# Attention backward, dV and dK: 32-row by 64-column matmul tiles and output tiles of one head per partition

## The chip, the core and the metric

The kernel runs on one core of one Trainium2 chip. The time is the device time of one execution in microseconds. Before the change it is 706.23 us, the median of three runs (704.14 to 710.16).

The core has a matrix engine (PE; its weight loads are listed apart as PEld), three engines for elementwise work (DVE, ACT, and POOL, which is GpSimd), a queue that only issues transfers here (SP), and 16 DMA engines that move data between HBM and the on-chip memory SBUF. Matmuls write PSUM, 8 banks of 512 fp32 values per partition, and ACT or DVE copy from there to SBUF.

## The reference

It is grouped-query attention with its gradients: 32 batches, 32 query heads with 4 queries each, 4 key/value heads, 2,048 keys, head size 128, all in bf16. Per batch and key/value head there are 8 x 4 = 32 query rows, so the four heads together fill 128 partitions.

```python
def _fwd_reference(q, k, v):
    ...
    scores = jnp.einsum("bhqd,bhkd->bhqk", q, k) * scale
    p = _softmax(scores, axis=-1)
    return jnp.einsum("bhqk,bhkd->bhqd", p, v)
...
def reference(q, k, v, grad_out):
    ...
    _out, _vjp = jax.vjp(_f, q, k, v)
    _grads = _vjp(grad_out)
    _out0 = jnp.asarray(_out)
    return (_out0, *[jnp.asarray(_g) for _g in _grads])
```

Written out per head, with e the exponentials and l their row sums: O = (e / l) V, dV = (e / l)^T dO, dS = e (dO V^T - delta) with delta the row sum of O dO, dQ = dS K scale / l, and dK = dS^T Q scale / l.

## The kernel before

One batch is some 60 steps, and the steps of several batches are interleaved in an order written out by hand: `STEADY` lists one round, where a suffix (`+`, `-`) says that a step belongs to a later or an earlier batch, and `TAIL` lists the last rounds. The engines carry out their instructions in the order in which these steps issue them; semaphores hold back an instruction whose input or buffer is not ready.

The steps of one batch:

- `LOAD` (L112): SP issues q, dO, four k and four v transfers of 512 KB. Key p x 16 + c lies in partition p, slot c, so a row of a transfer is 16 keys of one head, 4 KB. k has three buffers, v two; a load waits until PE is done with the old contents.
- `KT0..7`, `VT0..7` (L141 to L153): eight PE transposes each and a DVE copy. `QDT` does the same for q and dO.
- `Sa`, `Sb` (L155, L169): the scores; `EXa`, `EXb`: the exponentials on ACT; `NRM` (L197): 1/l on DVE, then on POOL dO / l (`dop`) and q scale / l (`qp`).
- `ETa/b`, `dSTa/b` (L208): transposes of e and dS; `O`, `dQ` (L222 to L253): gathers of 64 matmuls with 32 columns each, four column tiles at a time, and a small store on POOL's queue.
- `dPa`, `dPb` (L297): dO V^T on PE and dS on DVE.
- `dV0..7`, `dK0..7` (`outer`, L255): the pieces that the change is about. A piece covers two of the 16 key slots for all four heads. The array is used as two halves of 64 rows, and each half holds two heads. So that a half gives both heads side by side, `paired` (L190) lays `dop` and `qp` out as 256 columns, zero where the other head of the pair stands: four POOL operations of 32 partitions for each. A piece is four matmuls of 64 rows, 128 columns and 256 moving columns (L266); the two halves write one PSUM bank each. Then one copy of 128x1024 from PSUM to the output tile (L270), by ACT except where `TAIL` marks a step with `d`, for DVE.

The output tile of dV or dK has 128 partitions, 4 heads, 16 slots, 128 values: 32 KB per partition, three buffers for both. When its eight pieces are copied, POOL issues two stores of 1 MB, two heads each, in rows of 4 KB (L289). In the last batch half a tile leaves at a time, in one store each (L282). POOL's queue therefore holds, per batch, the `dop` and `qp` operations, the stores of O and dQ, and four large stores.

Of the kernel before, what the change touches and what calls it, by code (L numbers as in the profile page):

```python
# [9 lines left out]
BF16 = mybir.dt.bfloat16  # L10
ACT = mybir.ActivationFunctionType
ALU = mybir.AluOpType
# [49 lines left out]
def kernel(ctx: ExitStack, tc: tile.TileContext, q, k, v, grad_out, out_0, out_1, out_2, out_3):  # L62
    nc = tc.nc
    B, Hq, Sq, D = q.shape
    NH, Sk = k.shape[1], k.shape[2]
    P = 128
    G = Hq * Sq // NH
    C = Sk // P
    assert D == P and Hq * Sq == P and NH == 4 and G == 32 and C == 16
    scale = float(D) ** -0.5  # L70
    NZ = 3

    const = ctx.enter_context(tc.tile_pool(name="const", bufs=1))
    k_pool = ctx.enter_context(tc.tile_pool(name="kp", bufs=3))
# [7 lines left out]
    out_pool = ctx.enter_context(tc.tile_pool(name="outp", bufs=3))  # L82
    io_pool = ctx.enter_context(tc.tile_pool(name="iop", bufs=4))
    sm_pool = ctx.enter_context(tc.tile_pool(name="smp", bufs=3))
    ps_pool = ctx.enter_context(tc.tile_pool(name="ps", bufs=1, space=bass.MemoryType.PSUM))

    banks = Banks(ps_pool.tile([P, 8, 512], FP32, name="banks"))
# [3 lines left out]

    pairs = {}
    for x in ("dop", "qp"):
        for z in range(NZ):
            pairs[x, z] = const.tile([P, 2, D], BF16, name=f"{x}{z}")
            nc.gpsimd.memset(pairs[x, z][:], 0.0)

    q_f = q.rearrange("b h s d -> b (h s) d")  # L100
    go_f = grad_out.rearrange("b h s d -> b (h s) d")
    o_f = out_0.rearrange("b h s d -> b (h s) d")
    dq_f = out_1.rearrange("b h s d -> b (h s) d")
    k_v = k.rearrange("b h (p c) d -> b h p (c d)", c=C)
    v_v = v.rearrange("b h (p c) d -> b h p (c d)", c=C)
    dk_v = out_2.rearrange("b h (p c) d -> b p h (c d)", c=C)
    dv_v = out_3.rearrange("b h (p c) d -> b p h (c d)", c=C)

    store = nc.gpsimd
    st = {}  # L110
# [76 lines left out]
        )  # L187
        banks.give(t)

    def paired(S, name, src, by, b):  # L190
        t = pairs[name, b % NZ]
        for h in range(NH):
            r = slice(G * h, G * h + G)
            nc.gpsimd.tensor_scalar(out=t[r, h % 2, :], in0=src[r, :], scalar1=by[r, :], scalar2=None, op0=ALU.mult)  # L194
        S[name] = t

    def NRM(b):  # L197
        S = st[b]
        ls = sm_pool.tile([P, 1], FP32, name="ls")
        nc.vector.tensor_tensor(out=ls[:], in0=S["l"][:, 0:1], in1=S["l"][:, 1:2], op=ALU.add)  # L200
        S["rinv"] = sm_pool.tile([P, 1], FP32, name="rinv")
        nc.vector.reciprocal(out=S["rinv"][:], in_=ls[:])
        paired(S, "dop", S["do"], S["rinv"], b)
        S["srinv"] = sm_pool.tile([P, 1], FP32, name="srinv")
        nc.gpsimd.tensor_scalar_mul(out=S["srinv"][:], in0=S["rinv"][:], scalar1=scale)
        paired(S, "qp", S["q"], S["srinv"], b)

    def turned_rows(S, src, pool, name, i):  # L208
        t, ps = bank16()
# [44 lines left out]

    def outer(S, x, y, dst, name, i, b, copy):  # L255

        if name not in S:
            S[name + "left"] = 8
            S[name] = out_pool.tile([P, NH, C, D], BF16, name=name, tag="outp")
        t = banks.take(2)  # L260
        ps = banks.ap(t).rearrange("p a (j c d) -> p a j c d", j=2, c=2)
        for c in range(2):
            u = P * ((2 * i + c) % 8)
            for a in range(2):
                r = slice(2 * G * a, 2 * G * a + 2 * G)
                nc.tensor.matmul(  # L266
                    ps[:, a, :, c, :], lhsT=S[f"{x}{i // 4}"][r, u:u + P], rhs=S[y][r, :, :],
                    start=True, stop=True, tile_position=(2 * G * a, 0),
                )
        copy(  # L270
            out=S[name][:, :, 2 * i:2 * i + 2, :].rearrange("p h c d -> p h (c d)"),
            in_=banks.ap(t).rearrange("p a (j w) -> p (a j) w", j=2),
        )
        banks.give(t)
        S[name + "left"] -= 1
        if b == B - 1:

            half = f"{name}half{i // 4}"
            S[half] = S.get(half, 4) - 1
            if S[half] == 0:  # L280
                c = slice(8 * (i // 4), 8 * (i // 4) + 8)
                store.dma_start(  # L282
                    out=dst[b].rearrange("p h (c d) -> p h c d", d=D)[:, :, c, :].rearrange("p h c d -> p h (c d)"),
                    in_=S[name][:, :, c, :].rearrange("p h c d -> p h (c d)"),
                )
        elif S[name + "left"] == 0:
            o = S.pop(name)
            for a in range(2):
                store.dma_start(out=dst[b][:, 2 * a:2 * a + 2, :], in_=o[:, 2 * a:2 * a + 2].rearrange("p h c d -> p h (c d)"))  # L289

    def dV(b, i, copy=nc.scalar.copy):
        outer(st[b], "e", "dop", dv_v, "dv", i, b, copy)

    def dK(b, i, copy=nc.scalar.copy):
        outer(st[b], "ds", "qp", dk_v, "dk", i, b, copy)
# [21 lines left out]
    for w in STEADY.split():  # L317
        ahead = 0
        for mark, n in (("+3", 3), ("+2", 2), ("+", 1), ("-", -1)):
            if w.endswith(mark):  # L320
                w, ahead = w[:-len(mark)], n
# [3 lines left out]
    with tc.manual_schedule():  # L325
# [5 lines left out]
        for w in TAIL.split():  # L331
            w, b = w.split("@")
# [31 lines left out]
```

## Time and profile before

The page describes one profiled execution. Its span, first to last instruction, is 705.0 us, 1.2 us under the median of the three runs.

| | |
|---|---|
| median of three runs | 706.23 us |
| profiled execution, span | 705.0 us |
| chain that ended last | DMA 63%, PE 28%, DVE 3%, ACT 2% |
| L266 matmuls for dV, mean of one | 1,024, 274 ns |
| L266 matmuls for dK, mean of one | 1,024, 278 ns |
| L266 weight loads, mean of one | 94 to 95 ns |
| L270 copies on ACT, mean of one | 503, 1,021 to 1,026 ns |
| L194 `dop` and `qp` on POOL, mean of one | 256, 600 and 608 ns |
| L289 stores on POOL, mean of one issue | 124, 706 to 715 ns |
| k loads, v loads, issue to landing (median) | 13.9 us, 17.2 us |
| dV stores, dK stores, issue to landing (median) | 14.5 us, 11.1 us |

How to read it: a matmul's duration includes the time in which it passes through the array, so several are under way at once and the mean of one is not what it adds to the time; the distance between starts is. Busy shares are means over the whole span. DMA rates are given by slices of a fortieth of the span, 17.6 us each. A row of a timeline or of a chain gives start, length, engine, line, operation, output and input, and how many instructions were merged; in brackets stands the engine's idle time before it and what ended it.

### The profile page before, as it was taken

The page shows a single profiled execution, that of the slowest core. Times are in us where ns is not written, and L with a number is a line of the kernel's source. Part 1 is how long each engine was busy: PE and PEld are TensorE (multiplying, and loading weights), DVE is VectorE, ACT ScalarE, POOL GpSimd, SP SyncE. Part 2 cuts the span into 40 slices and gives each one's busy share as a digit, 9 for nine tenths or more (in the row PEclk, how much of TensorE's full clock was granted, in tenths as well). Part 3 has the DMA queues.
Part 4 walks back from the last instruction along what each step waited for, and adds up shares of the span by engine and source line. Part 5 has one row for each costly group of instructions (what it writes and reads, how often), then busy time and mean ns, then how long its engine had stood idle before and what let it go on. Part 6 is the DMA issues. An engine that isn't in the chain of part 4 may idle for free.

```text
span 705.0 us, 28195 instructions
## 1 busy us (share of the span) xinstructions
PE 634.6 (90%) x12352; PEld 458.4 (65%) x12352; DVE 596.3 (85%) x1001; ACT 560.6 (80%) x664; POOL 291.7 (41%) x492
## 2 busy tenths in 40 slices
PE   5899999799989799997999998979999989999893
PEld 4677777477767477764677766667666667666562
DVE  5999999789979869987788988859898879999983
ACT  0698898689879678886888897958988869887882
POOL 1445443344523444433444334533345443345451
PEclk9999999999999989999999999989999999999997
DMA  8999999999999999999999999999999999999867
GB/s 329 401 327 413 415 413 414 416 381 409 414 415 388 412 353 412 413 412 401 331 413 414 415 412 412 397 358 386 413 416 413 402 383 368 414 412 399 350 262 264
DMA packets 83067, 274.46 MB, mean 389 GB/s; under 512 B 16384, under 2 KB 16384, under 8 KB 82944
## 3 DMA queue, kind: packets, MB, share of 16 engines
q1 hardware_dynamic: 46080, 136.34, 50.0%
q0 software_dynamic: 36864, 136.33, 48.2%
q8 instruction: 96, 1.57, 0.8%
q14 instruction: 27, 0.22, 0.1%
HBM read 136.31 MB, written 136.31 MB: 387 GB/s over the span
## 4 chain that ended last, share of the span: by engine, by line
DMA 63%; PE 28%; DVE 3%; ACT 2%; issue 2%; POOL 1%; SPq 1%; POOLq 0%; ACTq 0%; DVEq 0%
DMA k_sb<-in_k_dram 27%; DMA v_sb<-in_v_dram 24%; PE banks L144 12%; DMA do_sb<-in_grad_out_dram 7%; PE banks L266 7%; PE banks L227 4%; PE banks L211 3%; PE banks L161 2%; DMA out_dram<-dk 2%; DMA out_dram<-dv 2%; ACT dv L270 1%; DVE ds L301 1%; POOL dop L194 1%; DVE dk L270 1%; DVE kt L146 1%
## 5 line engine op out<-in xcount | busy, mean ns | idle before, releaser
L270 ACT CAST dk<-banks 128x1024 bf16<-128x1024 f32 x249 | 244.1, 1021 | 56.5 <-PE banks L266 51.1
L270 ACT CAST dv<-banks 128x1024 bf16<-128x1024 f32 x254 | 243.7, 1026 | 45.8 <-PE banks L266 20.4
L146 DVE COPY kt<-banks 128x1024 bf16<-128x1024 bf16 x256 | 166.2, 684 | 28.3 <-PE banks L144 27.8
L144 PE MATMUL banks<-ident,k_sb 128*128 128x128 bf16 x2048 | 153.3, 227 | 28.2 <-DMA k_sb<-in_k_dram 24.5
L146 DVE COPY vt<-banks 128x1024 bf16<-128x1024 bf16 x256 | 166.9, 682 | 5.1 <-PE banks L144 4.6
L194 POOL TENSOR_SCALAR dop<-do_sb,rinv 32x128 bf16<-32x128 bf16 x128 | 76.8, 600 | 222.4 <-PE banks L266 147.5
L144 PEld LDWEIGHTS <-k_sb 128*128 128x128 bf16 x2048 | 126.4, 102 | 59.1 <-issue 30.3
L144 PE MATMUL banks<-ident,v_sb 128*128 128x128 bf16 x2048 | 144.9, 220 | 16.1 <-ACT dv L270 8.8
L144 PEld LDWEIGHTS <-v_sb 128*128 128x128 bf16 x2048 | 122.4, 98 | 33.1 <-issue 25.8
L266 PE MATMUL banks<-dop,e 64*128 64x256 bf16 x1024 | 98.3, 274 | 6.8 <-POOL dop L194 3.2
L289 POOL DMA_DIRECT2D out_dram<-dv x62 | 43.5, 706 | 136.8 <-ACT dv L270 136.8
L301 DVE SCALAR_TENSOR_TENSOR ds<-banks,delta,e 128x1024 bf16<-128x1024 f32 x64 | 82.1, 1284 | 14.1 <-PE banks L161 13.0
L266 PE MATMUL banks<-qp,ds 64*128 64x256 bf16 x1024 | 88.2, 278 | 1.7 <-DVE ds L301 0.6
L194 POOL TENSOR_SCALAR qp<-q_sb,srinv 32x128 bf16<-32x128 bf16 x128 | 77.8, 608 | 10.7
L185 ACT ACTIVATE e<-banks,negb 128x1024 bf16<-128x1024 f32 x64 | 70.8, 1110 | 9.6 <-DVE negb L177 9.5
L174 DVE TENSOR_REDUCE m<-banks 128x1 f32<-128x1024 f32 x64 | 75.2, 1217 | 1.9 <-PE banks L161 1.8
L266 PEld LDWEIGHTS <-e 64*128 64x128 bf16 x1024 | 34.0, 94 | 52.0 <-issue 34.5
L213 DVE COPY et<-banks 128x1024 bf16<-128x1024 bf16 x64 | 41.5, 686 | 28.0 <-PE banks L211 28.0
L266 PEld LDWEIGHTS <-ds 64*128 64x128 bf16 x1024 | 41.9, 95 | 31.3 <-ACT dv L270 12.7
L289 POOL DMA_DIRECT2D out_dram<-dk x62 | 44.1, 715 | 8.1 <-ACT dk L270 7.2
L213 DVE COPY dst<-banks 128x1024 bf16<-128x1024 bf16 x64 | 43.5, 683 | 0.0
L161 PE MATMUL banks<-vt,qdt 128*32 128x512 bf16 x512 | 40.9, 384 | 1.6 <-issue 1.6
(39 smaller groups left out, 477.9 us busy)
## 6 DMA issues: line engine op xcount, KB each, us to landing
k_sb<-in_k_dram SPq DMA_DIRECT2D x128, 512.0 KB, 13.9
v_sb<-in_v_dram SPq DMA_DIRECT2D x128, 512.0 KB, 17.2
out_dram<-dv POOLq DMA_DIRECT2D x64, 1024.0 KB, 14.5
out_dram<-dk POOLq DMA_DIRECT2D x64, 1024.0 KB, 11.1
q_sb<-in_q_dram SPq DMA_DIRECT2D x32, 32.0 KB, 17.5
do_sb<-in_grad_out_dram SPq DMA_DIRECT2D x32, 32.0 KB, 17.2
out_dram<-o_sb POOLq DMA_DIRECT2D x32, 32.0 KB, 13.8
out_dram<-dq_sb POOLq DMA_DIRECT2D x32, 32.0 KB, 5.5
```

The lines of the kernel that those rows point to most:

```text
L144: nc.tensor.transpose(out=ps[:, 4 * hh + j, :], in_=S[which][:, 2 * (i % 2) + hh, 4 * (i // 2) + j, :], identity=ident[:])
L146: nc.vector.tensor_copy(out=S[f"{which}t{i}"][:], in_=ps)
L161: nc.tensor.matmul(ps[G * h:G * h + G, a, :], lhsT=S["qdt"][:, col, G * h:G * h + G], rhs=xt[:, 4 * (h % 2):4 * (h % 2) + 4, :].rearrange( ...
L174: nc.vector.reduce_max(out=S["m"][:, i:i + 1], in_=S[f"s{i}"][1], axis=AX.X)
L185: nc.scalar.activation(out=S[f"e{i}"][:], in_=ps, func=ACT.Exp, bias=S["negb"][:], scale=scale, accum_out=S["l"][:, i:i + 1],)
L194: nc.gpsimd.tensor_scalar(out=t[r, h % 2, :], in0=src[r, :], scalar1=by[r, :], scalar2=None, op0=ALU.mult)
L213: nc.vector.tensor_copy(out=S[f"{name}{i}"][:], in_=ps)
L227: nc.tensor.matmul(ps[G * h:G * h + G, :], lhsT=S[f"{xt}{c // 8}"][:, c % 8, G * h:G * h + G], rhs=S[kv][:, h, c, :], start=(c == 0), stop ...
L266: nc.tensor.matmul(ps[:, a, :, c, :], lhsT=S[f"{x}{i // 4}"][r, u:u + P], rhs=S[y][r, :, :], start=True, stop=True, tile_position=(2 * G * ...
L270: copy(out=S[name][:, :, 2 * i:2 * i + 2, :].rearrange("p h c d -> p h (c d)"), in_=banks.ap(t).rearrange("p a (j w) -> p (a j) w", j=2),)
L289: store.dma_start(out=dst[b][:, 2 * a:2 * a + 2, :], in_=o[:, 2 * a:2 * a + 2].rearrange("p h c d -> p h (c d)"))
L301: nc.vector.scalar_tensor_tensor(out=S[f"ds{i}"][:], in0=ps, scalar=S["delta"][:], in1=S[f"e{i}"][:], op0=ALU.subtract, op1=ALU.mult,)
```

## The change

A piece no longer covers two key slots of 128 keys each, but four slots of 64 keys. The array is used in row quarters of 32 rows, one head each, and column halves of 64 columns: heads 0 and 2 use the left half, which writes partitions 0 to 63, heads 1 and 3 the right half, partitions 64 to 127. Heads 0 and 1 write the first PSUM bank of the piece, heads 2 and 3 the second. A piece is 16 matmuls of 32 rows, 64 columns and 128 moving columns. The 64 keys are every second column of a slot of e or dS.

An output tile then holds, in partition 64 a + p and for j = 0, 1, the 32 consecutive keys 32 p to 32 p + 31 of head 2 j + a: rows of 8 KB. POOL still issues two stores of 1 MB per tile, one for each j. In the last batch a half tile leaves in two stores of 512 KB in place of one of 1 MB, with rows of 2 KB as before. `dop` and `qp` are plain 128x128 tiles with one POOL operation each; the zeroed pairs and their six memsets are gone. The step order is the same. PE has 36,994 instructions in place of 24,706.

```diff
-    pairs = {}
-    for x in ("dop", "qp"):
-        for z in range(NZ):
-            pairs[x, z] = const.tile([P, 2, D], BF16, name=f"{x}{z}")
-            nc.gpsimd.memset(pairs[x, z][:], 0.0)
...
-    dk_v = out_2.rearrange("b h (p c) d -> b p h (c d)", c=C)
-    dv_v = out_3.rearrange("b h (p c) d -> b p h (c d)", c=C)
+    dk_v = out_2.rearrange("b (j a) (p c) d -> b j (a p) (c d)", a=2, c=R)
+    dv_v = out_3.rearrange("b (j a) (p c) d -> b j (a p) (c d)", a=2, c=R)
...
-    def paired(S, name, src, by, b):
-        t = pairs[name, b % NZ]
-        for h in range(NH):
-            r = slice(G * h, G * h + G)
-            nc.gpsimd.tensor_scalar(out=t[r, h % 2, :], in0=src[r, :], scalar1=by[r, :], scalar2=None, op0=ALU.mult)
-        S[name] = t
+    def scaled(S, name, src, by):
+        S[name] = sm_pool.tile([P, D], BF16, name=name)
+        nc.gpsimd.tensor_scalar(out=S[name][:], in0=src[:], scalar1=by[:], scalar2=None, op0=ALU.mult)
...
     def outer(S, x, y, dst, name, i, b, copy):
+        half, par, q4 = i // 4, (i % 4) // 2, 4 * (i % 2)
         if name not in S:
             S[name + "left"] = 8
-            S[name] = out_pool.tile([P, NH, C, D], BF16, name=name, tag="outp")
+            S[name] = out_pool.tile([P, 2, R, D], BF16, name=name, tag="outp")
         t = banks.take(2)
-        ps = banks.ap(t).rearrange("p a (j c d) -> p a j c d", j=2, c=2)
-        for c in range(2):
-            u = P * ((2 * i + c) % 8)
-            for a in range(2):
-                r = slice(2 * G * a, 2 * G * a + 2 * G)
+        ps = banks.ap(t).rearrange("p j (c d) -> p j c d", d=D)
+        x_v = S[f"{x}{half}"].rearrange("p (c k two) -> p c two k", two=2, k=64)
+        for c in range(4):
+            for h in range(NH):
+                j, a = divmod(h, 2)
+                r = slice(G * h, G * h + G)
                 nc.tensor.matmul(
-                    ps[:, a, :, c, :], lhsT=S[f"{x}{i // 4}"][r, u:u + P], rhs=S[y][r, :, :],
-                    start=True, stop=True, tile_position=(2 * G * a, 0),
+                    ps[64 * a:64 * a + 64, j, c, :], lhsT=x_v[r, q4 + c, par, :], rhs=S[y][r, :],
+                    start=True, stop=True, tile_position=(G * h, 64 * a),
                 )
+        c0 = C * par + 8 * half + q4
         copy(
-            out=S[name][:, :, 2 * i:2 * i + 2, :].rearrange("p h c d -> p h (c d)"),
-            in_=banks.ap(t).rearrange("p a (j w) -> p (a j) w", j=2),
+            out=S[name][:, :, c0:c0 + 4, :].rearrange("p j c d -> p j (c d)"),
+            in_=banks.ap(t),
         )
...
-            for a in range(2):
-                store.dma_start(out=dst[b][:, 2 * a:2 * a + 2, :], in_=o[:, 2 * a:2 * a + 2].rearrange("p h c d -> p h (c d)"))
+            for j in range(2):
+                store.dma_start(out=dst[b, j], in_=o[:, j].rearrange("p c d -> p (c d)"))
```

R is 32. The half stores of the last batch change in the same way.

More of the change, by code (lines that the diff above doesn't have):

```diff
@@ L70 @@
     scale = float(D) ** -0.5
-    NZ = 3
+    R = Sk // 64
+    assert R == 2 * C
     const = ctx.enter_context(tc.tile_pool(name="const", bufs=1))
@@ L202, in NRM @@
         nc.vector.reciprocal(out=S["rinv"][:], in_=ls[:])
-        paired(S, "dop", S["do"], S["rinv"], b)
+        scaled(S, "dop", S["do"], S["rinv"])
         S["srinv"] = sm_pool.tile([P, 1], FP32, name="srinv")
         nc.gpsimd.tensor_scalar_mul(out=S["srinv"][:], in0=S["rinv"][:], scalar1=scale)
-        paired(S, "qp", S["q"], S["srinv"], b)
+        scaled(S, "qp", S["q"], S["srinv"])
     def turned_rows(S, src, pool, name, i):
@@ L276, in outer @@
         if b == B - 1:
[L278 to L285, printed above, removed]
+            key = f"{name}half{half}"
+            S[key] = S.get(key, 4) - 1
+            if S[key] == 0:
+                c = slice(8 * half, 8 * half + 8)
+                for j in range(2):
+                    store.dma_start(
+                        out=dst[b, j].rearrange("p (two c d) -> p two c d", two=2, d=D)[:, :, c, :].rearrange("p two c d -> p two (c d)"),
+                        in_=S[name][:, j].rearrange("p (two c) d -> p two c d", two=2)[:, :, c, :].rearrange("p two c d -> p two (c d)"),
+                    )
         elif S[name + "left"] == 0:
             o = S.pop(name)
-            for a in range(2):
-                store.dma_start(out=dst[b][:, 2 * a:2 * a + 2, :], in_=o[:, 2 * a:2 * a + 2].rearrange("p h c d -> p h (c d)"))
+            for j in range(2):
+                store.dma_start(out=dst[b, j], in_=o[:, j].rearrange("p c d -> p (c d)"))
     def dV(b, i, copy=nc.scalar.copy):
```

## The prediction

> **What bounds the kernel now.** I read the page first (engines, slices, queues), then the busy table of one steady stage, the queue of GpSimd, the chain in order of time, the groups with shapes kept apart, and last single matmul and packet records.
>
> ```profile
> span 705.0 us, 28195 instructions
> PE 634.6 (90%) x12352; PEld 458.4 (65%) x12352; DVE 596.3 (85%) x1001; ACT 560.6 (80%) x664; POOL 291.7 (41%) x492
> ...
> GB/s 329 401 327 413 415 413 414 416 381 409 414 415 388 412 353 412 413 412 401 331 413 414 415 412 412 397 358 386 413 416 413 402 383 368 414 412 399 350 262 264
> DMA packets 83067, 274.46 MB, mean 389 GB/s; under 512 B 16384, under 2 KB 16384, under 8 KB 82944
> ...
> q1 hardware_dynamic: 46080, 136.34, 50.0%
> q0 software_dynamic: 36864, 136.33, 48.2%
> q8 instruction: 96, 1.57, 0.8%
> ```
>
> The transfers are the limit: the two data queues hold 98% of the 16 DMA engines. Most slices run at about 414 GB/s. Summing each slice's shortfall from 414 times its 17.6 us, over 414, the first slice loses 3.6 us, slices 2 to 37 together 23 us, the last three 15.6 us; 705.0 - 42 is 274.46 MB at 414 GB/s, so nothing else is lost.
>
> ```profile
> 60.00:140.00 80.00, 73.82 (x1444) 52.92 (x1444) 70.58 (x121) 68.17 (x82) 36.34 (x60) 1.00 1.03 414
> ```
>
> That is a full stage (columns: PE, PEld, DVE, ACT, POOL busy, clock, DMA share, GB/s). PE is 92% busy there, so it stands close behind. How close shows in the GpSimd queue of the same stage:
>
> ```profile
> 100.03 2.63 POOL L194 TENSOR_SCALAR dop<-do_sb,rinv 32x128 bf16<-32x128 bf16 x4 [6.15 <-PE banks L266]
> 102.75 0.21 POOL L205 TENSOR_SCALAR srinv<-rinv 128x1 f32<-128x1 f32 x1
> 103.06 2.71 POOL L194 TENSOR_SCALAR qp<-q_sb,srinv 32x128 bf16<-32x128 bf16 x4
> 105.83 0.62 POOL L253 DMA_DIRECT2D out_dram<-dq_sb  x1
> 106.46 1.42 POOL L289 DMA_DIRECT2D out_dram<-dk  x2
> ...
> 119.94 2.63 POOL L194 TENSOR_SCALAR dop<-do_sb,rinv 32x128 bf16<-32x128 bf16 x4 [6.22 <-PE banks L266]
> ```
>
> The computation takes 19.9 us a batch (119.94 - 100.03). The transfers need (274.46 - 1.79 MB of instruction fetch) / 32 = 8.52 MB, or 20.6 us at 414. They fall 0.7 us behind per batch; about every fifth batch PE runs out of k (it waits 24.5 us for k in 18 places), and while it catches up no buffer comes free and the DMA engines thin out. Those are the dips, some 108 us apart.
>
> **Stores.** 31 batches x 4 stores x 256 rows of 4 KB are 31,744 packets, and become 15,872 rows of 8 KB. In the packet records the median is 84 ns for 2,048 B and 159 for 4,096; the quiet 8,192 B packets of the instruction queue took 309. That is 9 ns fixed plus 36.6 ns per KB. If each 8 KB row goes as one packet, 15,872 x 9 ns / 16 = 8.9 us of all engines is saved. But with a share of 1.03 the records overlap by 3%, 5 of 159 ns, so 9 - 5 = 4 ns is the lower bound: 4.0 us. I take the middle, -6.5 us; the bounds are -8.9 and 0 (rival A).
>
> **PE.** Each of 512 pieces goes from 4 matmuls (two 64-row halves of 256 columns at once) to 16 (four 32-row quarters of 128 columns at once, if they overlap). The trace has no 32x64 tile; the nearest row is the gather L227, also four small tiles per step with a weight load each:
>
> ```profile
> 40.58 0.76 PE banks L266 x12
> ...
> 44.67 1.01 PE banks L227 x64
> ...
> 46.59 0.32 PE banks L266 x4
> ```
>
> (chain in order of time: start, length.) The gather does 16 steps of four in 1.01 us, 63 ns a step; single starts are 56 ns apart from step to step, 3 ns within one. Four such steps are 0.22 to 0.25 us. A piece today is 0.25 us in a run of three (0.76 / 3); its pairs start 109 ns apart, so 0.22 without the change of tile shape. I take no difference. The sure part is weight data: per partition 64 columns per step, against 128 in the gather. Bounds: from 0.03 us less a piece to 0.3 (the rivals); any more up to (20.6 - 19.9) / 16 = 0.04 us a piece is covered by the transfers, and if that cover is gone PE becomes the bound.
>
> **Instruction fetch.** 6,144 more matmuls and as many loads are 12,288 instructions. The instruction queue's 96 packets carry 1.57 MB for 24,704 PE instructions, 64 B each, so 48 more packets. By the queue's share, 0.8% x 16 x 705.0 / 96 = 0.94 us each: 48 x 0.94 / 16 = 2.8 us; by bytes at 414, 1.9. I take +2.5.
>
> **GpSimd.** Eight L194 operations of 32 rows (600 and 608 ns) become two of 128 rows. Nearest row: the same 128 elements per partition, so 0.6 us; at worst four times that, no gain. From 5.4 us a batch it falls to 1.4. dq and dk stores queue behind these (above), dv behind dk, so they are issued up to 4 us sooner. In full stages this changes nothing, as the DMA queue is never empty; what is late next there is still k. It counts at the first dop (22.2 to 24.9 us, on the chain): -1 us of a possible 2. The six memsets, 1.7 us, lie under the first loads: nothing. The 124 stores issue half the rows; from 0.71 us toward the 0.57 to 0.61 of the 128-row stores, hidden likewise.
>
> **Dips.** The transfers' net -6.5 + 2.5 = -4 us is 0.125 us a batch, so the lag falls from 0.7 to 0.58, and dips come a sixth more rarely: 23 / 6 = 4 us. Bounds 0 and -8.
>
> **Copies and tail.** ACT and DVE copies keep 128x1024 elements (1021 to 1026 ns, 1219 on DVE): nothing. SP's loads and waits, and the order on every queue, are as before; no wait is added. In the last batch four stores become eight on GpSimd, of 512 KB: one more issue of 0.75 us ahead of the last dq store, +0.5 (0 to 1.5).
>
> **Sum.** -6.5 + 2.5 + 0 - 1 - 4 + 0.5 = -8.5: a span of 696.5. The median of the three runs, 706.23, is 1.2 above the profiled span; so 698 us. Its own range, from the bounds, is 690 to 706.
>
> **Rival A, the store queue cuts its rows.** No packet of q0 is over 4,096 B. The 64 small stores (256 B rows) left as 1,024 packets of 2,048 B, eight rows joined, and half of the last batch's stores joined their 2 KB rows to 4,096. So this queue builds packets of up to 4 KB; an 8 KB row may leave as two, and the change then does not do what it says. For one packet: other queues do carry 8,192 and 16,384 B. Saving 0, fetch +2.5, head -1, tail +0.5: 707, with the 1.2 708.
>
> **Rival B, row quarters take turns at a bank (the slower side).** Of a step's four matmuls, heads 0 and 1 write halves of the partitions in the first bank, heads 2 and 3 in the second. Today the two row halves write separate banks, and the gather's four tiles share a bank but also all their rows. So no row here shows different row groups in one bank at the same time. If they take turns, only two of four overlap: 8 steps of 56 ns, 0.45 us a piece, +0.23, x16 = +3.6 us a batch. It decides above 0.04 us a piece. 23.5 us x 32 = 752, plus 705.0 - 32 x 20.6 = 46 for both ends and leftovers: 798, with the 1.2 799. Against it: the writes per partition are two streams at once in two banks, as now. The Trainium skill speaks for it: "TensorEngine Tiling (Array Packing)", section Restrictions and Gotchas, says that different row tiles cannot access the same PSUM bank simultaneously. By that rule the time would be this rival's; the trace before neither bears it out nor refutes it.
>
> **Rival C, the weight loads are not hidden.** A load's record lasts 94 to 99 ns whatever its shape. Gather and pieces hide it, but the gather loads only 32 columns per tile, and the pieces step every 109 ns. The new loads are 64 columns at every second element, every 56 ns. Fully bare, a step is 97 ns: +41 x 4 x 16 = +2.6 us a batch, 22.5 x 32 + 46 = 766; half bare 21.2 x 32 + 46 = 724. So 725 to 767. The same page of the Trainium skill, Tile-to-Partition Mapping, says that column tiling disables Fast Weight Load; "TensorE: Matmul & The Clock Gate", LDWEIGHTS, gives columns / 1.2 ns, which I estimate at 53 ns for 64 columns; with the four loads of a step in turn a step would be 213 ns and the time, by that estimate, about 1,000. The trace speaks against turns: the gather's four loads fit into 56 ns.
>
> **Chances.** Forecast 0.43, A 0.32, B 0.11, C 0.09, anything else 0.05. Overlap of tiles is well shown by the gather, so PE stays even at three in four; one packet or two is nearly open. The range must leave out at most 0.2: 690 to 745 leaves B, the upper half of C and 0.04 of the rest. About 1% (699.2 and 713.3) is what a measurement of this kernel tells from no change. Faster: 0.6 of the forecast, a fifth of A (if the earlier stores shorten dips), some of the rest: 0.34. Slower: B, C, a little of A and the rest: 0.24. Within: 0.42.
>
> **What would show it.** Stores: q0's packet count near 21,000 against 36,864, and a share below 48.2%. If the count stays, A. PE: L266's group of 8,192 matmuls, and the chain's pieces of x16 at 0.32 us or less; 0.55 would be B, 0.4 to 0.5 C, with DMA slices below 400 throughout and PE in place of DMA at the head of the chain. Fetch: q8 near 144 packets. Dips: fewer slices under 390 between the ends. GpSimd: 64 dop and qp operations near 0.6 us. The forecast is wrong if the full slices stay at 414 with fewer packets (the fixed 9 ns was hidden), or if store packets twice as long hold up the loads and the waits for k grow.

## The result and the profile after

The changed kernel takes 871.51 us, the median of four runs (863.73 to 879.76), against 707.14 for the kernel before on the same chip: a ratio of 1.229, with a 95% interval of 1.224 to 1.235. The ratio leaves out the run of 879.76 us, which fell into the slower of two states that executions show. The prediction was 698 with a range of 690 to 745.

These are the lines of the page after that answer to those shown of before:

```profile
span 867.0 us, 40289 instructions
PE 686.0 (79%) x18496; PEld 542.1 (63%) x18496; DVE 602.5 (69%) x1001; ACT 567.7 (65%) x664; POOL 154.1 (18%) x298
...
GB/s 348 347 352 279 346 288 364 348 268 319 301 309 368 282 290 371 328 344 289 312 309 374 303 342 293 311 343 301 354 278 360 300 338 352 333 317 271 277 293 193
...
q1 hardware_dynamic: 46080, 136.34, 44.6%
q0 software_dynamic: 21056, 136.33, 39.7%
q8 instruction: 144, 2.36, 1.0%
...
PE 69%; issue 18%; ACT 6%; DMA 3%; DVE 1%; SPq 1%; POOL 0%; POOLq 0%; ACTq 0%; DVEq 0%
```

The data queues are no longer full (84% of the engines, from 98%), and the chain went from DMA to PE. Yet PE is less busy as a share, 79% against 90%. What is new is "issue", 18% of the chain: time in which an engine waited for nothing that the profile shows. The waits of PE say where it sits (line waiting, releaser: total us, times, longest). In the kernel before, the chain and the longest waits of PE for "issue" were:

```profile
DMA 63%; PE 28%; DVE 3%; ACT 2%; issue 2%; POOL 1%; SPq 1%; POOLq 0%; ACTq 0%; DVEq 0%
...
PE banks L144 <- issue: 6.2, 13, 0.9
...
PE banks L266 <- issue: 2.9, 8, 0.5
```

In the changed kernel the waits are:

```profile
PE banks L264 <- issue: 63.6, 33, 3.8
PE banks L221 <- issue: 55.4, 30, 2.9
PE banks L141 <- issue: 17.1, 15, 2.8
PE banks L158 <- issue: 10.6, 4, 4.2
```

It does not belong to the new pieces (L264) alone; the gather (L221), whose code did not change, has nearly as much. In time order (start, length, matmuls merged, idle time before) one such pause stands in the middle of a piece:

```profile
308.95 0.42 PE L264 MATMUL banks<-qp,ds 32*64 32x128 bf16 x16
309.30 1.08 PE L221 MATMUL banks<-k_sb,dst 128*32 128x128 bf16 x64
310.31 0.85 PE L264 MATMUL banks<-qp,ds 32*64 32x128 bf16 x45
313.24 0.32 PE L264 MATMUL banks<-qp,ds 32*64 32x128 bf16 x3 [2.08 <-issue]
```

45 matmuls of three pieces run, then nothing for 2.1 us, then the other three. No semaphore, input tile or bank changes between the 45th and the 46th matmul. Before it the pieces run as forecast: from 308.95 to 309.30 a whole one.

The next view tells what the pauses have in common. It counts PE's instructions between the ends of consecutive pauses (the count of matmuls is the x behind the second number, that of weight loads behind the third):

```profile
313.24:336.65 23.41, 20.09 (x512) 16.24 (x512) 18.40 (x31) 15.70 (x18) 4.09 (x9) 0.93 0.88 322
336.65:348.24 11.59, 8.77 (x256) 7.46 (x256) 5.71 (x10) 6.97 (x8) 2.22 (x5) 0.82 0.91 315
348.24:365.71 17.47, 15.94 (x384) 12.30 (x384) 12.94 (x21) 12.93 (x16) 2.11 (x5) 0.83 0.89 329
365.71:372.19 6.48, 4.38 (x128) 3.92 (x128) 3.68 (x6) 3.25 (x4) 1.67 (x4) 1.00 0.81 305
372.19:378.11 5.92, 4.59 (x128) 3.02 (x128) 5.01 (x8) 3.85 (x4) 0.89 (x2) 1.00 0.98 339
378.11:391.09 12.98, 9.87 (x256) 7.77 (x256) 9.67 (x17) 9.00 (x11) 2.49 (x5) 1.00 0.87 343
```

Always a multiple of 128 matmuls and 128 loads: 256 instructions of 64 B, 16 KB, which is the size of a packet of the instruction queue. So PE pauses for its own code. The single records of the trace give the steps, as medians over the run: after PE has begun a block, 3.6 us pass until the packet with the next block starts, the packet takes 0.95 us, and 1.4 us after its end PE goes on. That is 6.0 us a block; 144 blocks are 864 us, the span is 867. That the two come so near each other is in part luck, since the blocks that ended in a pause took 3.3 to 8.4 us from beginning to beginning (median 6.2). Of the 113 blocks with fewer than 6 us of work in them 84 ended in a pause, of the 30 others 5. At 89 of the boundaries, then, PE stands still (the starts on both sides lie over 0.3 us apart), 172 us in all, and at each of the 89 it goes on 1.2 to 1.6 us after the end of an instruction packet; before, it was 27 boundaries and 18 us. The difference, 154 us, is nearly the 162 us by which the span grew.

The long pauses also go with a lower clock: the second and third rows above have granted clocks of 0.82 and 0.83 (the column after the five engines). In the trace the clock is halved in 31 stretches, 127 us in all (7 stretches and 39 us before); 30 of the 31 begin within 5 us of the start of a pause of 1.8 us or more, and in them transposes start 107 ns apart in place of 56. How much of this reaches the end was not measured: a block that must wait for the next one anyway hides it.

The Trainium skill has this in "Runtime: NRT & Kernel Launch", section Instruction fetch mechanics: instructions are refilled in blocks of 16 KiB, 256 instructions, and the next is fetched while the current one executes. The runs agree with both. It also calls the cost of crossing a boundary mostly hidden; here it was not, at 172 us.

### The profile page after: what moved, and what is told of

Same layout as the page of the kernel before. It is cut to its first block, busy times and chain, and to the rows that moved or that the text cites. A ratio compares the mean times of both kernels' runs of the same rounds, so it can differ in the third digit from the quotient of the medians.

```text
span 867.0 us, 40289 instructions
## 1 busy us (share of the span) xinstructions
PE 686.0 (79%) x18496; PEld 542.1 (63%) x18496; DVE 602.5 (69%) x1001; ACT 567.7 (65%) x664; POOL 154.1 (18%) x298
## 4 chain that ended last, share of the span: by engine, by line
PE 69%; issue 18%; ACT 6%; DMA 3%; DVE 1%; SPq 1%; POOL 0%; POOLq 0%; ACTq 0%; DVEq 0%
PE banks L141 29%; PE banks L264 18%; PE banks L205 8%; PE banks L221 8%; PE banks L158 6%; ACT dv L269 5%; DMA k_sb<-in_k_dram 2%; ACT dk L269 1%; DMA v_sb<-in_v_dram 1%; PE banks L131 1%; SPq L120 0%; DVE m L171 0%; DVE ds L300 0%; DVE vt L143 0%; SPq L117 0%
## 5 line engine op out<-in xcount | busy, mean ns | idle before, releaser
L141 PE MATMUL banks<-ident,v_sb 128*128 128x128 bf16 x2048 | 154.4, 228 | 15.0 <-issue 7.1
L264 PE MATMUL banks<-dop,e 32*64 32x128 bf16 x4096 | 113.9, 234 | 32.0 <-issue 31.6
L264 PEld LDWEIGHTS <-e 32*64 32x64 bf16 x4096 | 72.6, 113 | 83.6 <-issue 69.2
L264 PE MATMUL banks<-qp,ds 32*64 32x128 bf16 x4096 | 96.9, 224 | 33.7 <-issue 32.0
L264 PEld LDWEIGHTS <-ds 32*64 32x64 bf16 x4096 | 69.1, 109 | 57.6 <-issue 35.6
L288 POOL DMA_DIRECT2D out_dram<-dv x62 | 32.7, 532 | 249.9 <-ACT dv L269 249.7
L288 POOL DMA_DIRECT2D out_dram<-dk x62 | 33.1, 538 | 171.2 <-ACT dk L269 168.8
L221 PE MATMUL banks<-k_sb,dst 128*32 128x128 bf16 x2048 | 38.0, 221 | 29.1 <-issue 28.1
L221 PE MATMUL banks<-v_sb,et 128*32 128x128 bf16 x2048 | 38.2, 221 | 27.3 <-issue 27.3
L189 POOL TENSOR_SCALAR dop<-do_sb,rinv 128x128 bf16<-128x128 bf16 x32 | 19.3, 603 | 214.3 <-issue 73.4
```

The costliest lines, as they stand in the source:

```text
L141: nc.tensor.transpose(out=ps[:, 4 * hh + j, :], in_=S[which][:, 2 * (i % 2) + hh, 4 * (i // 2) + j, :], identity=ident[:])
L221: nc.tensor.matmul(ps[G * h:G * h + G, :], lhsT=S[f"{xt}{c // 8}"][:, c % 8, G * h:G * h + G], rhs=S[kv][:, h, c, :], start=(c == 0), stop ...
L264: nc.tensor.matmul(ps[64 * a:64 * a + 64, j, c, :], lhsT=x_v[r, q4 + c, par, :], rhs=S[y][r, :], start=True, stop=True, tile_position=(G * ...
L288: store.dma_start(out=dst[b, j], in_=o[:, j].rearrange("p c d -> p (c d)"))
```

## The experiments

The theory, called F: PE's code comes in blocks of 256 instructions, one block ahead, and the 6 us of a block bound the kernel. The rivals: T, the new tiles of 32 rows and 64 columns slow PE themselves; P, the store packets of 8 KB hold up the fetch.

**The changed kernel with a quarter of the matmuls.** One matmul of 512 moving columns per head, the 128 read four times over.

```diff
-        for c in range(4):
-            for h in range(NH):
+        for h in range(NH):
...
-                    ps[64 * a:64 * a + 64, j, c, :], lhsT=x_v[r, q4 + c, par, :], rhs=S[y][r, :],
+                ps[64 * a:64 * a + 64, j, :, :], lhsT=x_v[r, q4, par, :], rhs=S[y][r, None, :].to_broadcast([G, 4, D]),
```

> The changed kernel, but each piece has one matmul per head of 512 moving columns (dop or qp read four times over) in place of four of 128: slots 1 to 3 of a piece repeat slot 0, so three quarters of dV and dK are left out. Tiles, banks, PSUM writes, array time (213 against 224 ns a piece), copies, 8 KB stores stay; PE has 24,706 instructions as before the change. Theory F (PE's instructions come in blocks of 256, the next block is asked for only when the last begins, and needs about 5.9 us to be usable; 36,994 instructions are 144 blocks x 5.9 = 850 us): about 698, 690 to 707, few waits for 'issue' over 0.7 us. Rival T (the row-quarter, half-column tiles slow PE themselves): stays over 800. Rival P (8 KB store packets hold up the instruction fetch): 720 to 800.

Measured: 706.57 us, a ratio of 0.997 (0.994 to 1.000). 96 instruction packets, and PE pauses at 24 boundaries for 19 us. The new tiles, banks, store rows and operations are all in it, and the 165 us are gone: T and P fall, as far as the large cost goes. The time lies in F's range of 690 to 707, at its upper end; the forecast of 698 was too low by 9, which is taken up below.

**The kernel before with 16 matmuls a piece.** The reverse: the old layout, stores and GpSimd operations with the changed kernel's instruction count, in tiles of 64 rows and 64 columns with 128 moving columns.

```diff
-            for a in range(2):
-                r = slice(2 * G * a, 2 * G * a + 2 * G)
+            for j in range(2):
+                for m in range(2):
+                    for a in range(2):
+                        r = slice(2 * G * a, 2 * G * a + 2 * G)
...
-                    ps[:, a, :, c, :], lhsT=S[f"{x}{i // 4}"][r, u:u + P], rhs=S[y][r, :, :],
-                    start=True, stop=True, tile_position=(2 * G * a, 0),
+                            ps[64 * m:64 * m + 64, a, j, c, :], lhsT=S[f"{x}{i // 4}"][r, u + 64 * m:u + 64 * m + 64], rhs=S[y][r, j, :],
+                            start=True, stop=True, tile_position=(2 * G * a, 64 * m),
```

> The kernel before, same layout, 4 KB store rows, padded pairs and eight GpSimd operations, but each piece is 16 matmuls of 64 rows, 64 columns and 128 moving columns (four tiles at once) in place of 4: 36,994 PE instructions, same array time by the 56 ns step. The output is the reference's. Theory F: 870, 850 to 890, with PE stalls at every second block of 256. Rival T: 707 to 715, since no row quarter is used. Rival P: 707 to 760, since no packet is over 4 KB.

Measured: 862.39 us, 1.219 (1.213 to 1.226). Its page shows the same picture with 4 KB stores and the old tiles:

```profile
q0 software_dynamic: 36864, 136.33, 40.9%
q8 instruction: 144, 2.36, 1.0%
...
PE 70%; issue 18%; ACT 6%; DMA 3%; POOL 1%; DVE 1%; SPq 1%; POOLq 0%; ACTq 0%; DVEq 0%
```

PE pauses at 90 boundaries for 164 us, and the median from a block's beginning to its packet is 3.5 us, against 3.6 with 8 KB packets. The instruction count makes the slowdown, without row quarters and without rows of 8 KB. The half-width tiles, which this run shares with the changed kernel, were in the first experiment too and cost nothing there.

**The same with 8 matmuls a piece**, 256 moving columns each, again on the kernel before.

```diff
-            for a in range(2):
-                r = slice(2 * G * a, 2 * G * a + 2 * G)
+            for m in range(2):
+                for a in range(2):
+                    r = slice(2 * G * a, 2 * G * a + 2 * G)
...
-                    ps[:, a, :, c, :], lhsT=S[f"{x}{i // 4}"][r, u:u + P], rhs=S[y][r, :, :],
-                    start=True, stop=True, tile_position=(2 * G * a, 0),
+                        ps[64 * m:64 * m + 64, a, :, c, :], lhsT=S[f"{x}{i // 4}"][r, u + 64 * m:u + 64 * m + 64], rhs=S[y][r, :, :],
+                        start=True, stop=True, tile_position=(2 * G * a, 64 * m),
```

> As the last, but 8 matmuls of 64 rows, 64 columns and 256 moving columns a piece: 28,802 PE instructions, 112.5 blocks. Theory F: 112.5 x 5.9 = 664 lies under the 707 of before, so only stretches with dense instructions stall: 710 to 740. Rivals T and P: 707 to 712.

Measured: 725.66 us, 1.025 (1.019 to 1.030), inside F's 710 to 740. PE pauses at 51 boundaries for 68 us, 50 us more than before, and 18 us of it reach the end. 112 blocks of 6.0 us would fit into the time, so the average does not bind. The dense blocks do: 51 of the 70 with under 6 us of work ended in a pause, and none of the other 41. Part of what they lose the transfers cover.

**The changed kernel without large stores** in the first 31 batches, which leaves these outputs out.

```diff
-            o = S.pop(name)
-            for j in range(2):
-                store.dma_start(out=dst[b, j], in_=o[:, j].rearrange("p c d -> p (c d)"))
+            S.pop(name)
```

> The changed kernel without the dV and dK stores of the first 31 batches (these outputs are left out). Theory F with the fetch waiting in the DMA engines behind data packets: the time from asking to arrival falls from 3.6 us to under 2, a block needs some 4 us, 144 x 4 = 576 is under the work of PE itself: 660 to 720. If the 5.9 us are a fixed cost of the fetch whatever the engines carry: 840 to 870.

Measured: 767.47 us, the median of two runs, 1.083 (1.074 to 1.091), between the two cases. The instruction packets are still 144, and the mean rate of all transfers falls from 317 to 191 GB/s:

```profile
DMA  8864445644366545466354666545466534664214
...
q0 software_dynamic: 3200, 6.30, 2.3%
q8 instruction: 144, 2.36, 1.2%
```

The pauses fall from 172 to 85 us. The wait from a block's beginning to its packet falls from 3.6 to 1.2 us, but this median runs over two kinds of blocks, because the loads come in bursts with idle DMA engines between them. Where the data queues held under 10% of the engines within 0.5 us of the beginning (76 blocks), the median wait was 0.8 us; at the other 67 it was 3.5 us, as in the changed kernel, and 36 of the 45 pauses with 76 of the 85 us stand there. The changed kernel has the same two kinds: 1.1 us at 19 blocks with idle engines, 3.7 at the other 124. So the wait is mostly time behind data packets, about 2.7 of the 6.0 us, and is no fixed cost; with idle engines some 3.2 us remain of a block (0.8 + 1.0 + 1.4). The expectation missed because it took one short wait for all blocks, while the loads still hold up the fetch.

**GpSimd's part alone, on the kernel before.** `dop` and `qp` by two operations of 128 rows, with a 0/1 mask, in place of four of 32.

```diff
+    mask = const.tile([P, 2], FP32, name="mask")
...
-        for h in range(NH):
-            r = slice(G * h, G * h + G)
-            nc.gpsimd.tensor_scalar(out=t[r, h % 2, :], in0=src[r, :], scalar1=by[r, :], scalar2=None, op0=ALU.mult)
+        m = sm_pool.tile([P, 2], FP32, name=name + "m")
+        nc.gpsimd.tensor_scalar(out=m[:], in0=mask[:], scalar1=by[:], scalar2=None, op0=ALU.mult)
+        for j in range(2):
+            nc.gpsimd.tensor_scalar(out=t[:, j, :], in0=src[:], scalar1=m[:, j:j + 1], scalar2=None, op0=ALU.mult)
```

> The kernel before with GpSimd's part lightened alone: dop and qp are each written by two operations of 128 rows (the scale times a 0/1 mask per head parity) after one of 128x2, in place of four of 32 rows. The output is the reference's; 4 KB store rows, 24,706 PE instructions. If the earlier stores and the earlier first dop are worth what the prediction gave them (1 us at the head and a share of the dips): 703 to 706. If GpSimd is off the path: 707, within 0.3%.

Measured: 703.81 us, 0.996 (0.994 to 0.998), against 705.97 for the kernel before in these rounds. This small part of the change is a gain, and it leaves nothing out: this version is faster than both kernels, than the one before by 0.2 to 0.6%. Where the gain lies is taken up below.

**Quarter of the matmuls, store rows of 4 KB.** The first experiment with each tile stored in four parts.

```diff
             for j in range(2):
-                store.dma_start(out=dst[b, j], in_=o[:, j].rearrange("p c d -> p (c d)"))
+                for w in range(2):
+                    store.dma_start(
+                        out=dst[b, j][:, C * D * w:C * D * w + C * D],
+                        in_=o[:, j, C * w:C * w + C, :].rearrange("p c d -> p (c d)"),
+                    )
```

> The run with four matmuls per piece (slots 1 to 3 repeat slot 0, so three quarters of dV and dK are left out), but each tile leaves in four stores of 512 KB with rows of 4 KB in place of two of 1 MB with rows of 8 KB. If the fixed 9 ns of a store packet counts: 6 to 9 us above the 706.6 of the 8 KB rows. If it is hidden under other packets (full stages there ran at 413 GB/s with half the packets): 706 to 708.

Measured: 702.28 us, 0.994 (0.992 to 0.996), below both expected ranges, which were set from 706.6 us on another chip; the ratios compare. The rows of 4 KB are not slower than those of 8 KB (0.997, 0.994 to 1.000, on another chip); from the far ends of the two intervals, longer rows gain at most 0.3%. The stage from 60 to 140 us, same columns as in the prediction, first with 8 KB rows:

```profile
60.00:140.00 80.00, 76.23 (x1484) 52.01 (x1480) 71.59 (x123) 70.15 (x83) 18.67 (x36) 1.00 1.02 413
```

and with 4 KB rows:

```profile
60.00:140.00 80.00, 76.34 (x1454) 52.13 (x1452) 71.63 (x121) 69.01 (x82) 26.47 (x52) 0.98 1.03 414
```

413 and 414 GB/s. In this stage half as many store packets move no more bytes per us. Over the profiled executions, one each, PE waits 32.3 us for k in 27 places with rows of 8 KB, and 24.7 us in 15 with rows of 4 KB.

**Two matmuls a piece on the kernel before**, 512 moving columns, the second slot repeating the first.

```diff
-        for c in range(2):
-            u = P * ((2 * i + c) % 8)
+        u = P * ((2 * i) % 8)
...
+                rhs=S[y][r].rearrange("p j d -> p (j d)")[:, None, :].to_broadcast([2 * G, 2, 2 * D]),
```

> The kernel before with two matmuls per piece of 512 moving columns (the 256 read twice), so the second slot of a piece repeats the first and half of dV and dK is left out: 20,610 PE instructions, 80.5 blocks. The block boundaries cost PE 18 us in the profile of before. If the transfers cover them: 703 to 708. If the instruction fetch already bounds part of before: 690 to 700.

Measured: 704.31 us, 0.998 (0.995 to 1.000). The pauses fall from 18 to 8 us, and at most 0.5% of the time, 3 us, with them. In the kernel before, the transfers cover most of the fetch.

**GpSimd's part, with q and dO loaded through GpSimd's queue.** The edit of the lighter GpSimd part, and in addition:

```diff
-        nc.sync.dma_start(out=S["q"][:], in_=q_f[b])
+        nc.gpsimd.dma_start(out=S["q"][:], in_=q_f[b])
...
-        nc.sync.dma_start(out=S["do"][:], in_=go_f[b])
+        nc.gpsimd.dma_start(out=S["do"][:], in_=go_f[b])
```

> The kernel before with the lighter GpSimd part, and q and dO loaded through GpSimd's queue, which joined rows of 256 B into packets of 2 KB when it stored O and dQ: 8,192 packets of 18 ns become 1,024 of 84. The output is the reference's. If a packet's fixed cost counts: 3.9 us of all engines less, 702 to 704. If it is hidden: 706 to 708; if these loads now wait behind the stores and delay the transposes: above 710.

Measured: 883.76 us, 1.251 (1.248 to 1.254): the last of the three cases, and far beyond it. The rows are a wait of PE and GpSimd's queue in time order:

```profile
PE banks L139 <- DMA q_sb<-in_q_dram: 173.5, 30, 9.2
```

```profile
321.50 1.42 POOL L295 DMA_DIRECT2D out_dram<-dk  x2 [2.08 <-ACT dk L276]
322.92 0.56 POOL L245 DMA_DIRECT2D out_dram<-o_sb  x1
323.46 0.56 POOL L120 DMA_DIRECT2D q_sb<-in_q_dram  x1
```

The load of q in these rows is issued behind the dK stores, which wait for ACT's copies, and PE waits 173.5 us for q in 30 places. What a packet's fixed cost is worth for these loads stays open; the delay buries it.

## Why the prediction was wrong

**PE's pieces: right.** Four tiles overlap; single starts within a run are 56 ns from step to step, as in the gather. A piece takes 0.35 us from its start to the next step's (308.95 to 309.30) and two in a row 0.57, against 0.32 and 0.54 before: the second step of a piece starts 82 ns after the first and not 67 as in the gather (medians), which the wider loads may explain; no run tests it. Rivals B and C fall: row quarters that share a bank do not take turns, so the rule of the Trainium skill ("TensorEngine Tiling (Array Packing)", Restrictions and Gotchas) that different row tiles cannot access one PSUM bank at the same time does not hold here, with 56 ns a step, where they write different partitions of it; and 64-column loads hide behind a step of 56 ns.

**Instruction fetch: the step that failed.** It was priced as traffic, 48 packets more, 2.5 us of the DMA engines. The count was right (144 packets) and the price nearly so (3.2 us in the packet records), but the packets have a latency that PE must wait out, one block at a time; this term the sum put at nothing. The profile of before held the parts: 96 packets over 705 us are one per 7.3 us, and PE stood still at 27 block boundaries. Half as many instructions again leave 705 / 144 = 4.9 us a block; the question whether a block can be had in that time was not asked, and none of the rivals stood for it. The experiment with 16 matmuls on the old layout showed it in its place: 862 us with the new count and 164 us of pauses at block boundaries.

**Stores: the mechanism right, the size wrong.** The queue carried 15,872 packets of 8,192 B, median 309 ns, so rival A falls too. But the 6.5 us (4.0 to 8.9) did not come. In the first experiment the store packets' records did shrink, from 332 to 325 us for each engine (packets of 4 and 8 KB), while the load packets' grew from 340 to 345. In the full stage nothing of the fixed 9 ns was gained: 413 against 414 GB/s. The prediction named this as what would make it wrong, and also that the waits for k might grow, which they did there, from 24.5 to 32.3 us. One reading under rival A was off, without weight: all of the last batch's stores left in joined packets, not half (32,768 packets of 4,096 B are the 31,744 and 1,024 for its 4 MB).

**GpSimd and the dips: the operations right, their worth mis-sized.** The operations took 0.60 us each. Alone, they are worth 0.4% (0.2 to 0.6), 3 us, where the prediction had 1 us, at the head. The page of that run has this row:

```profile
GB/s 332 404 340 413 414 413 414 416 376 412 414 415 414 357 411 414 413 413 387 331 413 414 415 416 369 409 414 411 410 379 354 414 414 414 416 341 337 359 347 259
```

Summed as in the prediction, the first slice loses 3.5 us (3.6 before), slices 2 to 37 lose 25 (23) and the last three 12 (16). So in this one execution the gain stands at the end, and neither at the head, where the prediction had it, nor in the dips; why, no run shows.

**The rest of the sum.** Without its instructions the change gives 0.3% (0.0 to 0.6), about 2 us, where the sum without fetch had 11. Nearly all of this gap is the stores and the dips that were to become rarer with them; slices 2 to 37 of the first experiment lose 26 us, not less than the 23 of before.

## What to carry to other kernels

Count the instructions of an engine per 256 and ask how long each block works: in the changed kernel 84 of 113 blocks with under 6 us of work ended in a pause, wherever their instructions came from, and nearly all the pauses stood where the DMA engines were busy with data. Smaller tiles that cost the array nothing still multiply the code, and pauses "for nothing that the profile shows", at fixed distances in instructions, are its sign. Before making DMA packets fewer and longer, look whether the full stages already run at one steady rate: here they did, and half as many store packets gained nothing.

## What the runs showed of the hardware

The refill of PE's code shares the DMA engines with the data: without the large stores its wait was 0.8 us at the blocks that began with idle engines, and 3.5 us at the others. Pauses of PE of some 2 us and more were often followed by 3.4 us or more at half the granted clock. Packets of one queue of 8,192 B took 309 ns where two of 4,096 took 318, and yet the rate was the same. Four tiles of 32 rows and 64 columns, two in each bank, ran as fast as four column tiles of 128 rows, 56 ns from step to step.
